# Another fixed order and other PSUM banks for the same 3284 tasks of a threshold-attention and mixer kernel

## The chip, the cores and the metric

The kernel runs on one core of one Trainium2 chip. The metric is the device time of one execution in microseconds, the median over runs; lower is better. Engines are named as in the profile: PE (matrix products; PEld its weight loads), DVE (vector), ACT (scalar), POOL (GpSimd), SP (sync, which here only issues DMAs).

## The reference

Attention over 8 batches, 8 heads, 576 rows, 64 columns, with a threshold in place of a plain softmax, and then a mixer with a low-rank part over the rows and two dense layers over 512 channels:

```python
scores = scale * np.matmul(q, k.transpose(0, 1, 3, 2))
thresh = np.max(scores, axis=-1, keepdims=True) - tau
scores = np.where(scores >= thresh, scores, -1000000000.0)
scores = scores - np.max(scores, axis=-1, keepdims=True)
attn = np.exp(scores)
attn = attn / (np.sum(attn, axis=-1, keepdims=True) + 1e-09)
x = np.matmul(attn, v)          # then heads side by side: (8, 576, 512)
...
xt = x.transpose(0, 2, 1)
h = xt @ U @ V                  # U: 576 x 32, V: 32 x 576
u = x + h.transpose(0, 2, 1)
out = u + np.maximum(u @ w_ch1, 0.0) @ w_ch2    # 512 -> 2048 -> 512
```

Inputs and output are fp32.

## The kernel before

**Pairs and steps.** Two heads of one batch are a pair; there are 32 pairs, numbered 0 to 31, four to a batch. The 576 rows of a head are four tiles of 128 and one of 64; the fifth tiles of two neighbouring pairs go together, so that two pairs have nine score steps. A score step writes two tiles of 128x576 scores (one for each head, j) into PSUM. Pairs 0 and 1, and the first step of every later two pairs, have single steps; else two steps are issued as one double step (`score_tasks`, L620).

**What one step goes through.** PE multiplies queries and keys in fp32 (L637); DVE scales a tile into SBUF and takes its minimum, since the sign is turned ("weighing", L666); ACT makes the threshold (L682) and the exponential (L689); DVE keeps what passes the threshold and sums it ("selection", L696). The weights are bf16; they are transposed by a DMA on SP's queue (L720) or, for some early tiles, by PE and an eviction on ACT (L727, L737), after POOL has copied their last 64 columns (L714). PE multiplies them with the values, which are split into a high and a low bf16 part (L796, L800, L804); DVE, ACT and POOL divide by the sums (L827, L851 to L862).

**Before a pair's first step** its queries and keys are loaded in eight parts (L506: five or four groups of 64 rows x 64 columns for 64 partitions, 80 or 64 KB), transposed by PE in fp32 (L568, L581) and copied to SBUF by ACT (L574, L587). Pairs 0 to 2 load mostly on SP's queue, later ones on POOL's. Values are loaded on SP's queue (L530).

**After a pair** come the low-rank products (L875, L890), the sum u on DVE (L897) and its transposition (L912 on PE for pairs 0 to 7, later by DMA). When the four pairs of a batch are done its mixer may start: 16 up-projections of four products (L994), with a relu on ACT (L984), and 16 down-projections of four (L1027), an addition on DVE (L1039) and the stores (L1050 to L1056). Odd batches carry the fifth tiles of two batches besides (L1010).

**What sets the order.** The work is cut into 3284 tasks, each with an engine, what it needs and a function that issues its instructions. They are numbered as they are made. `Order.run` (L352) goes through a table of numbers, `ORDER` (L130), and issues each task in that order; each engine so gets its own queue in the table's order, and semaphores hold an instruction until what it needs is there. A negative number issues an idle product of zeros into a bank (`fill`, L468): -3 into bank 2, -6 into bank 5.

```python
for n in ORDER:
    if n < 0:
        self.filler(-1 - n)
        continue
    t = self.tasks[n]
```

**Banks.** PSUM has eight banks. Banks 0 to 2 are the tile `trio0`, 3 to 5 `trio1`, 6 and 7 tiles of their own. A single score step takes banks 0, 1, 3 and 4, a double one 0 to 5. Every other task of PE that writes PSUM takes the one bank that the table `BANK` (L299) gives it. `BankOrder` (L10) makes the waits by banks: an access waits for the last access to the same bank from another engine.

Of the kernel before, what the change touches and what calls it, by code (L numbers as in the profile page):

```python
# [112 lines left out]
class Task:  # L113
# [17 lines left out]
    24, 22, 21, 26, 20, 23, 19, 25, 29, 42, 43, 28, 46, 27, -3, -3, -3, -3, -3, -3, -3, -3, -3, -3, -3, -3, -3, -3, 30, 39, 34, 31, 32,  # L131
    40, 35, 33, 45, -3, -3, 59, 41, 204, 60, 48, 61, 63, 205, -3, -3, -3, -3, -3, -3, 69, 62, 36, 47, 64, 65, 44, 37,
    70, 38, 203, 71, 73, 201, 1, 66, -3, -3, -3, -3, -3, -3, 82, 72, 199, 77, 3, 74, 202, 67, 52, 83, 200, 54, 50, 68,
    84, 86, 0, 78, -3, 95, 85, 90, 198, 87, 53, 208, 224, 51, 96, 55, 79, 88, 97, -3, -3, -3, 80, 75, 221, 76, 91,
    108, 98, 99, 2, 81, 49, 211, 109, 103, 89, 110, 104, -3, -3, -3, -3, 119, 111, 207, 219, 112, 220, 100, 114, 209,
    225, 120, 101, 121, 92, 102, 123, 222, 115, -6, -6, -6, -6, -6, 129, 125, 223, 113, 122, 218, 93, 130, 213, 118,
    94, 435, 131, 214, 212, 116, 439, 126, 117, 142, 132, 56, 434, 124, 137, 169, 57, 206, 143, 133, 58, 144, 146,
    168, 4, -6, 155, 210, 227, 138, 150, 127, 170, 229, 145, 433, 128, 156, 231, 105, 157, 437, 106, 232, 228, 438,
    151, 107, 238, 158, 226, 134, 163, 233, 230, 239, 456, 234, 159, -6, 171, 240, 135, 457, 136, 147, 241, 455, 173,
    164, 242, 459, 248, 160, 215, 458, 244, 165, 172, 139, 152, 174, 148, 250, 175, 436, 149, 140, 166, 249, 216, 161,  # L140
    217, 262, 251, 162, 256, 261, 167, 454, 245, 440, 273, 141, 432, 243, 252, 263, 257, 268, 246, 274, 264, 452, 247,
    275, -8, -8, 153, 258, 453, 176, 184, 253, 177, 442, 281, 183, 254, 154, 5, 286, 255, 277, 6, -4, 188, 185, 265,
    276, 259, 186, 260, 287, 266, 267, 189, 445, 282, 296, 446, 269, 283, 187, 291, 278, 288, 235, 447, 297, 284, 279,
    280, 289, 292, 236, 443, 285, 298, 441, 622, 190, 290, 619, 448, 302, 178, 306, 295, 345, 625, 444, 307, 293, 300,
    237, 294, 191, 344, 179, 192, 318, 308, 299, 626, 313, 346, 460, 301, 7, 180, 462, 319, 620, 309, 465, 270, 320,
    322, 624, 271, 303, 463, 466, 623, 181, 272, 310, 304, 321, 347, 464, 331, 311, 305, 182, 314, 326, 349, 348, 334,
    467, 315, 312, 193, 350, 316, 323, 351, 332, 317, 324, 461, -4, -4, 352, 642, 194, 353, 325, 640, 354, 327, 195,
    472, 646, 333, 355, 339, 8, 196, 335, 356, 468, 473, 197, -6, 357, 336, 328, 337, 621, 474, 364, 338, 9, 340, 476,
    482, 643, 475, 359, 358, 639, 477, 449, 341, 483, 478, 342, 450, 365, 329, 343, 484, 360, 330, 495, 485, 362, 486,
    496, 11, 498, 479, 645, 507, 497, 10, 487, 469, 480, 502, 363, 488, 361, 451, 508, 366, 634, 632, 509, 644, 511,  # L150
    627, 520, 367, 633, 629, 630, 368, 521, 635, 481, 631, 374, 886, 369, 499, 490, 530, 883, 370, 489, 523, 641, 491,
    371, 500, 532, 628, 515, 492, 372, 882, 501, 503, 493, 373, 470, 510, 376, 531, 494, 504, 525, 512, 13, 386, 377,
    887, 516, 378, 533, 534, 513, 541, 881, 514, 380, 387, 540, 12, 522, 379, 382, 375, 536, 524, 505, 383, 384, 535,
    506, 552, 381, 526, 543, 537, 527, 385, 553, 547, 471, 528, 650, 554, 542, 556, 388, 538, 565, 888, 539, 651, 390,
    560, 566, 517, 15, 394, 548, 885, 391, 529, 389, 544, 518, 555, 659, 572, 561, 545, 395, 396, 549, 568, 546, 661,
    16, 884, 660, 392, 397, 647, 557, 519, 550, 649, 669, 567, 393, 569, 551, 573, 570, 665, 670, 663, 562, 571, 578,
    558, 574, 671, 673, 398, 682, 677, 648, 683, 559, 579, 652, 672, 399, 654, 580, 402, 905, 678, 655, 662, 653, 563,
    14, 664, 575, 403, 400, 904, 564, 666, 901, 576, 694, 577, 902, 685, 674, 908, 401, 689, 695, 581, 892, 667, 684,
    696, 903, 896, 894, 893, 707, 582, 895, 1052, 708, 698, 675, 586, 679, 690, 668, 583, 599, 587, 897, 584, 636,
    691, 686, 585, 717, 676, 600, 697, 588, 710, 601, 589, 598, 709, 18, 699, 712, 17, 718, 590, 603, 700, 637, 701,  # L160
    719, 702, 638, 680, 727, 406, 604, 681, 602, 605, 890, 607, 728, 407, 606, 404, 608, 656, 687, 609, 906, 688, 713,
    692, 729, 591, 405, 1054, 765, 711, 592, 693, 907, 703, 734, 593, 610, 739, 594, 766, 714, 611, 657, 767, 715,
    704, 658, 595, 740, 723, 612, 716, 1048, 912, 752, 613, 720, 911, 596, 1055, 705, 735, 597, 408, 706, 741, 409,
    721, 724, 913, 614, 722, 410, 730, 615, 747, 725, 411, 736, 726, 731, 743, 914, 753, 616, 769, 732, 910, 742, 412,
    754, 915, 617, 891, 744, 773, 618, 733, 737, 770, 748, 745, 921, 774, 759, 764, 749, 889, 775, 755, 771, 794, 776,
    923, 746, 738, 772, 750, 414, 922, 1053, 751, 413, 756, 1049, 916, 917, 931, 795, 925, 760, 757, 927, 796, 1072,
    785, 758, 924, 932, 768, 786, 933, 761, 777, 909, 1050, 926, 415, 935, 1051, 942, 762, 1071, 787, 416, 934, 763,
    941, 1069, 778, 788, 1074, 417, 928, 779, 898, 1068, 780, 936, 946, 950, 929, 418, 944, 797, 930, 789, 781, 937,
    899, 951, 782, 900, 419, 790, 952, 960, 1061, 791, 1059, 954, 792, 783, 938, 793, 1063, 1062, 420, 943, 961, 918,
    421, 939, 947, 953, 1070, 940, 784, 422, 1064, 1277, 945, 1060, 956, 1274, 955, 1058, 970, 798, 1273, 957, 919,  # L170
    962, 963, 972, 1279, 965, 799, 971, 423, 948, 1278, 800, 949, 981, 974, 801, 1280, 426, 802, 973, 1275, 976, 424,
    806, 427, 958, 803, 1276, 959, 807, 1009, 975, 808, 977, 804, 428, 805, 966, 978, 429, 980, 985, 1075, 979, 809,
    1010, 1073, 811, 430, 982, 810, 1011, 431, 986, 989, 812, 964, 1056, 983, 967, 990, 920, 968, 813, 991, 993, 1013,
    999, 992, 814, 1057, 1000, 995, 425, 843, 994, 1004, 1079, 984, 1014, 969, 1081, 844, 1015, 1088, 1082, 987, 1008,
    988, 1080, 996, 1016, 1002, 815, 1089, 1001, 1077, 1012, 817, 1090, 816, 997, 1092, 1005, 998, 1017, 1091, 819,
    1003, 818, 1018, 1094, 1083, 1019, 1098, 1093, 1293, 1084, 820, 1028, 1020, 1095, 1297, 1021, 1006, 1100, 1065,
    1296, 821, 1007, 1099, 1294, 1037, 822, 1109, 1066, 1029, 1038, 1299, 1104, 1039, 1108, 1096, 1022, 1030, 1097,
    823, 1101, 1031, 1023, 1102, 1105, 1032, 1024, 1111, 1117, 1076, 1025, 824, 1295, 1078, 1103, 1113, 1067, 1118,
    1110, 1288, 1284, 1119, 1289, 1121, 1106, 1286, 1283, 1127, 845, 1285, 1107, 1446, 1128, 1120, 1287, 1033, 1447,
    1122, 1123, 1298, 1282, 1112, 1137, 1034, 1300, 1281, 846, 1114, 1441, 1130, 1035, 1040, 1085, 1138, 1440, 827,  # L180
    1132, 1139, 1086, 1141, 1442, 825, 1124, 828, 1115, 847, 1147, 1140, 1036, 1129, 1116, 826, 1148, 1125, 829, 1041,
    1133, 1126, 1143, 1156, 1131, 830, 1149, 1142, 1134, 848, 1152, 1157, 1087, 1135, 1304, 1150, 1158, 831, 1305,
    1443, 1166, 835, 1301, 1444, 1144, 1042, 1167, 1176, 1145, 1043, 836, 1146, 1151, 832, 1308, 1313, 1309, 1153,
    1159, 1162, 1154, 1177, 1306, 1315, 1160, 1155, 833, 1467, 1314, 1307, 1180, 1460, 834, 1163, 1136, 1169, 1445,
    1178, 1044, 1161, 1464, 1323, 1181, 1026, 1463, 1045, 1319, 1027, 1175, 1466, 1317, 1182, 1164, 1324, 1184, 1171,
    1179, 1165, 1204, 1325, 1183, 1168, 837, 1461, 1205, 1170, 1185, 839, 1186, 1327, 1206, 1187, 1333, 1462, 841,
    840, 1334, 838, 849, 1172, 1316, 842, 1320, 1173, 1342, 850, 1326, 1195, 1329, 1174, 1318, 1290, 1328, 1321, 1188,
# [975 lines left out]
```

## Time and profile before

| | |
|---|---|
| runs | 590.59, 591.26, 592.37 us; median 591.26 |
| the profiled execution's own time | 590.78 us |
| its span in the profile | 589.0 us |
| PE busy | 568.7 us, 97% |
| DVE busy | 509.9 us, 87% |
| ACT busy | 460.2 us, 78% |
| POOL busy | 331.7 us, 56% |
| chain of work that ended last | PE 56% of the span, DVE 2%, issue 1% |
| granted clock of PE in the 40 slices | 9 tenths or more in each |

The busy time of an engine counts its instructions and not its queue's. The ends of PE's products are modelled, so neighbouring ones overlap by some 0.17 us and an idle time of PE is shown too short. The waits are put down to what came last. Lines such as L637 are those of the kernel before; in the changed kernel the table is one line longer, so that L637 there is L638.

### The profile page before, as it was taken

The numbers are of one execution on the slowest core, as the hardware profiler recorded it, in microseconds if no ns is written. First come the engines' busy times: TensorE is split into PE (matmuls) and PEld (weight loads), VectorE is DVE, ScalarE is ACT, GpSimd is POOL, SyncE is SP. The second block draws the span as 40 slices with busy tenths as digits, with TensorE's granted clock in tenths as the row PEclk, the third lists the DMA queues.
The fourth block names the chain that finished last, engine by engine and source line by source line (L and its number), as shares of the span: only waits on it lengthen the run. The fifth ranks groups of instructions, "written<-read, shape, count | busy, mean of one in ns | idle before, by whom it ended". The sixth has DMA issues, their size and how long they took to land.

```text
span 589.0 us, 16929 instructions
## 1 busy us (share of the span) xinstructions
PE 568.7 (97%) x6142; PEld 345.8 (59%) x6214; DVE 509.9 (87%) x1400; ACT 460.2 (78%) x959; POOL 331.7 (56%) x580
## 2 busy tenths in 40 slices
PE   9898899999999999999999999999999999999996
PEld 3456655765666665555566665655665746556553
DVE  4999999999999999999998999999899799953101
ACT  4688999998899977998788987799877896774430
POOL 3887775968576748764666765566645551341000
PEclk9999999999999999999999999999999999999999
DMA  5999999969999999998989989999898798672303
GB/s 134 170 166 182 179 133 175 188 113 176 193 155 186 147 173 203 165 175 166 159 166 173 188 147 198 162 188 186 142 175 165 122 167 168 134 117 46 72 1 90
DMA packets 226996, 90.49 MB, mean 154 GB/s; under 512 B 205408, under 2 KB 217520, under 8 KB 226912
## 3 DMA queue, kind: packets, MB, share of 16 engines
q1 hardware_dynamic: 212544, 67.48, 70.5%
q0 software_dynamic: 13408, 21.58, 19.8%
q8 instruction: 49, 0.80, 0.6%
q10 hardware_dynamic: 960, 0.34, 0.2%
q14 instruction: 35, 0.29, 0.2%
HBM read 37.90 MB, written 9.44 MB: 80 GB/s over the span
## 4 chain that ended last, share of the span: by engine, by line
PE 56%; DVE 2%; issue 1%; ACT 0%
PE trio L637 13%; PE bank L1027 12%; PE trio L994 6%; PE bank L994 6%; PE trio L1027 4%; PE bank L800 4%; PE trio L800 3%; PE bank L1010 1%; PE bank L568 1%; PE trio L568 1%; DVE s_sb L666 1%; PE bank L875 1%; DVE w_ring L696 1%; PE bank L796 0%; PE trio L1010 0%
## 5 line engine op out<-in xcount | busy, mean ns | idle before, releaser
L689 ACT ACTIVATE e_sb<-s_sb,m 128x576 bf16<-128x576 f32 x288 | 217.5, 774 | 37.2 <-DVE s_sb L666 18.0
L696 DVE SCALAR_TENSOR_TENSOR w_ring<-s_sb,thr,e_sb 128x576 bf16<-128x576 f32 x288 | 229.7, 823 | 5.5 <-issue 1.5
L666 DVE TENSOR_SCALAR_CACHE_REDUCE s_sb<-trio 128x576 f32<-128x576 f32 x288 | 205.3, 749 | 9.3 <-PE trio L637 8.5
L637 PE MATMUL trio<-qkT 64*64 64x288 f32 (+2 forms) x2304 | 161.8, 410 | 2.1 <-DVE s_sb L666 1.6
L714 POOL COPY w_ring<-w_ring 128x128 bf16<-128x128 bf16 (+1 forms) x168 | 65.0, 395 | 115.3 <-DVE w_ring L696 71.7
L637 PEld LDWEIGHTS trio<-qkT 64*64 64x64 f32 x2304 | 81.4, 133 | 52.9 <-DVE s_sb L666 6.4
L1027 PE MATMUL bank<-W2b,R 128*128 128x512 bf16 x402 | 101.6, 380 | 1.9 <-issue 0.6
L506 POOL DMA_DIRECT2D qkraw<-in_k_dram x117 | 76.6, 656 | 25.9 <-PE trio L568 12.0
L1027 PEld LDWEIGHTS <-R 128*128 128x128 bf16 x576 | 53.1, 98 | 60.8 <-issue 9.1
L506 POOL DMA_DIRECT2D qkraw<-in_q_dram x117 | 76.4, 655 | 12.0 <-PE bank L581 3.0
L994 PEld LDWEIGHTS <-W1b 128*128 128x128 bf16 x512 | 46.7, 98 | 55.9 <-issue 10.9
L862 POOL TENSOR_TENSOR x<-x,rec 128x256 f32<-128x256 f32 (+1 forms) x84 | 52.7, 631 | 33.0 <-DVE x L855 21.8
L984 ACT ACTIVATE R<-bank 128x512 bf16<-128x512 f32 x80 | 47.2, 594 | 29.6 <-PE bank L994 16.4
L994 PE MATMUL bank<-uT,W1b 128*128 128x512 bf16 x244 | 66.6, 380 | 1.8 <-DVE x L855 0.2
L603 POOL TENSOR_TENSOR vh<-vraw_ring,vh 64x128 bf16<-64x128 f32 x64 | 53.5, 835 | 19.1 <-ACT vh L596 9.5
L800 PEld LDWEIGHTS <-wT_ring 128*128 128x128 bf16 x896 | 55.5, 98 | 9.9 <-issue 3.6
L994 PE MATMUL trio<-uT,W1b 128*128 128x512 bf16 x231 | 57.6, 379 | 0.4
L984 ACT ACTIVATE R<-trio 128x512 bf16<-128x512 f32 x64 | 37.5, 597 | 8.4 <-PE trio L994 8.0
L682 ACT ACTIVATE thr<-m,tau_t 128x2 f32<-128x2 f32 x144 | 41.5, 293 | 2.3 <-DVE s_sb L666 1.9
L1039 DVE TENSOR_TENSOR o<-bank,x 128x512 f32<-128x512 f32 x27 | 18.5, 686 | 27.5 <-PE bank L1027 27.2
L800 PE MATMUL bank<-vh,wT_ring 128*128 128x128 bf16 x496 | 35.6, 220 | 0.1
L1027 PE MATMUL trio<-W2b,R 128*128 128x512 bf16 x140 | 33.5, 379 | 0.3
(105 smaller groups left out, 719.6 us busy)
## 6 DMA issues: line engine op xcount, KB each, us to landing
out_dram<-o SPq DMA_DIRECT2D x71, 128.0 KB, 2.9
vraw_ring<-in_v_dram SPq DMA_DIRECT2D x32, 160.0 KB, 4.0
qkraw<-in_k_dram POOLq DMA_DIRECT2D x59, 80.0 KB, 4.2
qkraw<-in_q_dram POOLq DMA_DIRECT2D x58, 80.0 KB, 4.5
vraw_ring<-in_v_dram SPq DMA_DIRECT2D x32, 128.0 KB, 4.1
qkraw<-in_q_dram POOLq DMA_DIRECT2D x59, 64.0 KB, 4.2
qkraw<-in_k_dram POOLq DMA_DIRECT2D x58, 64.0 KB, 4.3
W1b<-in_moe_w_ch_dram POOLq DMA_DIRECT2D x8, 256.0 KB, 5.5
```

Of the source, the lines that this page charges most:

```text
L506: queue.dma_start(pr.qkraw[part, to, j, :], src[:, j, of, :])
L603: nc.gpsimd.tensor_tensor(out=pr.vh[part, tiles_, :, h, :], in0=raw[part, tiles_], in1=pr.vh[part, tiles_, :, 0, :], op=ALU.subtract)
L637: mm = nc.tensor.matmul(cols[part, lo:hi], a.tT[hs, 0, rows], a.tT[hs, 1, lo:hi], start=True, stop=True)
L666: nc.vector.tensor_scalar(out=s_sb, in0=score_cols(slot, x), scalar1=-scale, scalar2=None, op0=ALU.mult, op1=ALU.min, accum_out=m[:, x:x + 1])
L689: nc.scalar.activation(out=e_sb, in_=s_sb, func=ACT.Exp, bias=m[:, x:x + 1], scale=-1.0)
L696: nc.vector.scalar_tensor_tensor(out=w_sb[:, 0:S], in0=s_sb, scalar=thr_[:, x:x + 1], in1=e_sb, op0=ALU.is_le, op1=ALU.mult, accum_out=pr. ...
L714: nc.gpsimd.tensor_copy(out=w_sb[:, xs, S:640], in_=w_sb[:, xs, 512:S])
L800: nc.tensor.matmul(av[:, 2 * a + j, :], w, pr.vh[:, kt, j, :, :], start=kt == 0, stop=False)
L862: nc.gpsimd.tensor_tensor(out=x, in0=x, in1=over_sum(part), op=ALU.mult)
L984: nc.scalar.activation(out=R2[:, fts, lo:hi], in_=bank[t.got[0]].rearrange("p (f c) -> p f c", c=hi - lo), func=ACT.Relu)
L994: nc.tensor.matmul(bank[t.got[0]], W1b[:, dt, ft * P:(ft + 1) * P], bt.uT[:, dt, :], start=(dt == 0), stop=(dt == 3))
L1027: nc.tensor.matmul(ch, R2[:, ft, lo:lo + P], W2b[:, ft, :], start=(ft == 0), stop=(ft == 15))
```

## The change

The two tables are replaced. `ORDER` holds the same 3284 tasks, each of them moved by 13 places on average and by up to 289; 45 idle products instead of 49, 11 of them ahead of the first transposition instead of 14. `BANK` gives another bank to 277 of the 481 tasks that have one. All else is the same line for line: the tasks, what each needs, tiles, buffers, DMAs.

```diff
 ORDER = (
-    24, 22, 21, 26, 20, 23, 19, 25, 29, 42, 43, 28, 46, 27, -3, -3, -3, -3, -3, -3, -3, -3, -3, -3, -3, -3, -3, -3, 30, 39, 34, 31, 32,
...
+    25, 22, 21, 26, 19, 23, 20, 24, 46, 44, 29, 28, 40, -3, -3, -3, -3, -3, -3, -3, -3, -3, -3, -3, 30, 27, 32, 31, 34, 39,
...
 BANK = {n: b for b, tasks in {
     0: (
...
-        2449, 2496, 2514, 2635, 2665, 2817, 2819, 2825, 2837, 2849, 2857, 2906, 3190, 3224, 3228,),
...
+        2402, 2408, 2415, 2417, 2433, 2437, 2665, 2685, 2778, 2825, 3003, 3057, 3183, 3198, 3203, 3224, 3232, 3234,),
```

What it moves is read from the engines' queues. The names: `trio_159` and `trio_160` are trio0 and trio1, `bank_161` and `bank_162` banks 6 and 7; `qkraw_103` holds the raw queries and keys of even pairs, `qkraw_104` of odd ones; `qkT_105` and `qkT_106` the transposed ones; `w_ring` the weights; `R_163` the relu's output.

PE's queue between the first and the second score step of pair 1, before:

```order
L637 MATMUL trio_160<-qkT_106 64x288 x2
L568 MATMUL trio_159<-ident,qkraw_103 128x128 x4
L469 LDWEIGHTS zeros
L469 MATMUL trio_160<-zeros 128x512
...
L637 MATMUL trio_159<-qkT_106 64x288 x2
```

and now:

```order
L638 MATMUL trio_160<-qkT_106 64x288 x2
L569 MATMUL bank_161<-ident,qkraw_103 128x128 x4
L470 LDWEIGHTS zeros
L470 MATMUL trio_159<-zeros 128x512
L728 LDWEIGHTS w_ring_82
L728 MATMUL bank_162<-identb,w_ring_82 128x128
...
L638 MATMUL trio_159<-qkT_106 64x288 x2
```

Before, the pair of idle rows stands five times; now once, and the weight transposition's pair of rows five times. The query transpositions of pair 2 (the x4 row) stay; the key ones, which stood ahead of the first score step, are now behind the third.

SP's queue where the last query loads of pair 2 stand, before:

```order
L506 DMA qkraw_103<-in_k_dram 64x5x64
L506 DMA qkraw_103<-in_q_dram 64x4x64 x2
L506 DMA qkraw_103<-in_k_dram 64x4x64
L506 DMA qkraw_103<-in_q_dram 64x5x64
L720 DMA_TRANSPOSE wT_ring_84<-w_ring_80 128x10x128
L506 DMA qkraw_103<-in_q_dram 64x5x64
L530 DMA vraw_ring_88<-in_v_dram 64x2x64
```

and now:

```order
L507 DMA qkraw_103<-in_k_dram 64x5x64
L721 DMA_TRANSPOSE wT_ring_84<-w_ring_81 128x5x128
L507 DMA qkraw_103<-in_q_dram 64x5x64
L507 DMA qkraw_103<-in_q_dram 64x4x64
L721 DMA_TRANSPOSE wT_ring_84<-w_ring_80 128x10x128
L507 DMA qkraw_103<-in_k_dram 64x4x64
L531 DMA vraw_ring_88<-in_v_dram 64x2x320
L507 DMA qkraw_103<-in_k_dram 64x4x64
```

The last query load, 24th DMA of the queue, stood behind the ten-block transposition; now the last query load is the 23rd, behind a five-block one, and two key loads stand behind the ten-block one.

PE's queue at the end of pair 7's scores and, further on, before the second score step of pair 8, before:

```order
L875 MATMUL bank_162<-xb_ring_99,Ub 128x128
L568 MATMUL bank_161<-ident,qkraw_104 128x128 x4
L912 LDWEIGHTS ub_151
L912 MATMUL trio_159<-identb,ub_151 128x128
...
L727 MATMUL bank_162<-identb,w_ring_82 128x128
...
L1027 MATMUL bank_161<-W2b,R_163 128x512
L581 MATMUL trio_160<-ident,qkraw_104 128x128
L637 MATMUL trio_159<-qkT_105 64x288 x2
```

and now:

```order
L876 MATMUL bank_162<-xb_ring_99,Ub 128x128
L569 MATMUL bank_161<-ident,qkraw_104 128x128 x4
L1028 LDWEIGHTS R_163
L1028 MATMUL trio_159<-W2b,R_163 128x512
...
L728 MATMUL bank_161<-identb,w_ring_82 128x128
...
L582 MATMUL trio_159<-ident,qkraw_104 128x128
L801 LDWEIGHTS wT_86
L801 MATMUL bank_162<-vh_108,wT_86 128x128
...
L638 MATMUL trio_159<-qkT_105 64x288 x2
```

The weight transposition (L727) used the bank of the low-rank product (L875) shortly before; now it uses the bank of the fp32 transpositions, with twelve products of 512 columns (L1028) between. The transposition L581 stood right ahead of the double step; now ten small products stand between.

## Rows read from the trace of the kernel before

**Rows 1.** Busy time by stage; columns: stretch, its length, each engine's busy time, clock.

```profile
9.00:83.00 74.00, 64.92 (x962) 41.21 (x955) 71.64 (x201) 62.13 (x124) 57.32 (x105) 1.00 1.12 168
83.00:140.00 57.00, 55.96 (x642) 35.23 (x648) 55.92 (x156) 54.73 (x115) 42.00 (x77) 1.00 1.05 160
140.00:500.00 360.00, 356.35 (x3892) 220.30 (x3946) 345.05 (x951) 299.67 (x636) 216.66 (x371) 1.00 0.99 169
```

**Rows 2.** Timeline of PE, 78 to 84 us: start, duration, instruction, idle before.

```profile
83.07 1.02 PE L994 MATMUL bank<-uT,W1b 128*128 128x512 bf16 x3 [0.18 <-ACT uT L928]
```

**Rows 3.** Waits of DVE, 0 to 84 us: total, times, longest.

```profile
DVE s_sb L666 <- PE trio L637: 7.0, 2, 6.3
DVE x L827 <- PE bank L796: 0.4, 1, 0.4
```

**Rows 4.** Waits of PE, 140 to 589 us.

```profile
PE bank L1027 <- issue: 0.6, 4, 0.2
```

**Rows 5.** Timeline of PE at the opening.

```profile
0.99 4.85 PE L469 MATMUL trio<-zeros 128*128 128x512 bf16 x11 [0.99 <-DVE tau_t L397]
...
0.99 5.50 PE L469 MATMUL trio<-zeros 128*128 128x512 bf16 x14 [0.99 <-DVE tau_t L397]
...
6.33 0.61 PE L568 MATMUL trio<-ident,qkraw 128*128 128x128 f32 x4
```

**Rows 6.** DMA issues at 2.4 us: size, time to landing.

```profile
qkraw<-in_q_dram SPq DMA_DIRECT2D x1, 80.0 KB, 3.7
```

**Rows 7.** Timeline of PE, 15 to 48 us.

```profile
24.25 0.63 PE L568 MATMUL trio<-ident,qkraw 128*128 128x128 f32 x4 [0.78 <-issue]
...
24.71 1.24 PE L469 MATMUL trio<-zeros 128*128 128x512 bf16 x5
...
25.88 1.20 PE L637 MATMUL trio<-qkT 64*64 64x288 f32 x16
...
37.93 2.17 PE L637 MATMUL trio<-qkT 64*64 64x288 f32 x32
```

**Rows 8.** Timeline of DVE, 15 to 48 us.

```profile
23.28 0.07 DVE L696 DVE_READ_ACCUMULATOR w_ring<-s_sb,thr,e_sb 128x1 f32 x1
...
23.50 0.76 DVE L666 TENSOR_SCALAR_CACHE_REDUCE s_sb<-trio 128x576 f32<-128x576 f32 x1
...
27.12 0.76 DVE L666 TENSOR_SCALAR_CACHE_REDUCE s_sb<-trio 128x576 f32<-128x576 f32 x1 [0.69 <-PE trio L637]
...
39.72 0.74 DVE L666 TENSOR_SCALAR_CACHE_REDUCE s_sb<-trio 128x576 f32<-128x576 f32 x1
```

**Rows 9.** Timeline of SP's queue, 14 to 28 us.

```profile
16.55 2.30 SPq L720 DMA_TRANSPOSE wT_ring<-w_ring  x1
...
18.89 0.93 SPq L506 DMA_DIRECT2D qkraw<-in_q_dram  x1
...
20.63 1.23 SPq L720 DMA_TRANSPOSE wT_ring<-w_ring  x1
```

**Rows 10.** DMA issues at 18.9 us.

```profile
qkraw<-in_q_dram SPq DMA_DIRECT2D x1, 80.0 KB, 5.3
```

**Rows 11.** Timeline of PE, 119 to 137 us.

```profile
120.59 0.39 PE L912 MATMUL trio<-identb,ub 128*128 128x128 bf16 x4
...
121.28 0.44 PE L727 MATMUL bank<-identb,w_ring 128*128 128x128 bf16 x5 [0.30 <-ACT tt L881]
...
130.57 0.27 PE L581 MATMUL trio<-ident,qkraw 128*128 128x128 f32 x1
...
131.03 2.17 PE L637 MATMUL trio<-qkT 64*64 64x288 f32 x32 [0.19 <-DVE s_sb L666]
...
135.30 1.03 PE L1027 MATMUL bank<-W2b,R 128*128 128x512 bf16 x4
...
136.44 0.45 PE L875 MATMUL trio<-xb_ring,Ub 128*128 128x128 bf16 x5
```

**Rows 12.** Busy time by stage, the first idle products; last columns: clock, DMA share, GB/s.

```profile
0.90:5.60 4.70, 4.61 (x11) 1.66 (x12) 2.17 (x12) 1.49 (x2) 1.75 (x4) 1.00 0.59 140
```

385 rows, old and new, of tables (BANK, ORDER) are left out of this document.

## The prediction

> **What bounds the kernel now.** I read the busy time by stage first [rows 1]. From 9 to 83 us DVE is busy 71.64 of 74 us and PE 64.92; from 140 to 500 us PE is busy 356.35 of 360. So there are two stages. Up to 83.07 us, where the first up-projection of the mixer stands [rows 2], PE has only attention to work on and goes at DVE's pace; from there it has a store of mixer products and is the bound to the end. The tables of waits then say what is lost in each. DVE waits 7.0 us for scores in the first 84 us, of which 6.3 are the opening, so 0.7 later, and 0.4 us once for a product [rows 3]. After 140 us PE's longest entry is 0.6 us in four waits [rows 4].
>
> This bounds what any order of the same tasks can give. All products, evictions and loads stay. PE idles much before 83 us, but it gets work there only as fast as DVE makes selections; taking PE's waits away gives nothing unless DVE moves up. What is to be had is DVE's 74 − 71.64 = 2.4 us up to 83, PE's 57 − 55.96 = 1.0 us up to 140 [rows 1], the 0.6 us after that and a few tenths in the opening: some 4 us, 0.7% of the time.
>
> **The opening: 11 idle products, and other first loads.** Eleven idle products take 4.85 us and all fourteen 5.50 us from 0.99 us; the first transposition starts at 6.33 [rows 5]. Three products less free PE by 0.65 us. But that transposition also needs the last query load of pair 0, issued at about 2.4 us and 3.7 us under way [rows 6]: 6.1 us. With the same load at most 0.2 us is free. The change puts the 64 KB part last instead of the 80 KB part, which can land earlier: the upper bound is 0.6 us. Against it, two 80 KB loads of pair 1 follow at once where a 32 KB one stood; as lower bound I allow 0.2 us the other way. I take 0.1, since the load and not PE is last. In all the program has 45 idle products and not 49; the others stand before the first up-projection in PE's spare time, so they cost and give nothing while DVE is the pace there; if it were not, four at 0.21 us, 0.8 us.
>
> **The late query load of pair 2.** This is the one large loss of DVE's stage. After the first score step of pair 1 PE stands at the query transpositions of pair 2 until 24.25 us, 0.78 us idle for nothing that the profile names; behind them come five idle products from 24.71, and only then, at 25.88, the next score step [rows 7]. DVE idles 0.69 us until 27.12 for that step, and 0.15 us (23.28 + 0.07 to 23.50) for the one before [rows 8]. The cause is on SP's queue: the load was issued at 18.89, behind a DMA transposition of ten blocks that held SP 2.30 us from 16.55 [rows 9], and took 5.3 us [rows 10]: 24.2 us.
>
> Three things move here. The last query load stands one place earlier on SP, behind a transposition of five blocks and not of ten (1.23 us in place of 2.30 [rows 9]), so I put its issue 1.1 + 0.4 us earlier, near 17.4, and its landing, again 5.3 us later, near 22.7. The key transpositions of pair 2, which stood ahead of the first score step of pair 1, now stand behind the third. And of five idle products between the query transpositions and the second score step one is left, with the five small products of a weight transposition. The first step then starts when DVE releases it, before 22.0, and ends (1.20 us) near 23.2; 0.5 us of transpositions, 0.2 and 0.3 us later PE is at the second step, at 24.2. DVE needs two weighings of at most 0.76 us from 23.3 to release its banks, so PE is no longer last, and the 0.69 + 0.15 = 0.84 us go. Bounds: nothing, if the load is as late as before; 1.2 with the 0.4 us for a product [rows 3]. I take 0.84, as the issue moves by more than PE's 0.78 us of waiting. What is late next there is DVE itself. This moves up the first up-projection and all that PE does after.
>
> **Waits of PE from 83 to 140 us.** Three have one pattern: a product writes a bank that ACT or DVE still reads. At 121.28 a weight transposition waits for the copy of a low-rank product of the same bank, with 0.7 us of PE work between; at 131.03 a double score step stands right behind a transposition into one of its own banks; at 136.44 a low-rank product uses a bank of the score steps [rows 11]. The ends there are modelled, so I count from start to start, a product of 512 columns at 0.21 us (five take 1.24, four 1.03 [rows 7, 11]), a small one at 0.06 (0.45 less 0.39), a transposition of fp32 at 0.11: 0.45, 0.35 and 0.3 us, 1.1 in all; the idle listed is 0.5. In the change twelve products of 0.21 us stand ahead of that weight transposition, ten small ones between that transposition and the double step, and the low-rank product has another bank. All three should go. A new order has waits of its own: between 0.1 us (57 us of the stretch after, 0.6 us in 449) and 1.1. I take 0.4, nearer to the long quiet stretch. Net 0.7; bounds 1.0 and 0.
>
> **After 140 us** the same is allowed for the new order, 0.6 us [rows 4], so the difference is nothing, with 0.6 us either way. The end is the same in both: the last products, a sum, two stores.
>
> **The sum.** 0.1 + 0.84 + 0.7 = 1.64 us off the profiled execution's own 590.78 us: 589.14. The median of the runs is 591.26, 0.48 above it; carried over, 589.6 us, 0.28% less than the median. A measurement of this kernel can tell about 0.3% (1.8 us) from no change, so this is no change, by a hair.
>
> **Row and rule on the clock.** The first eleven idle products take 0.44 us each and the three behind them 0.22 (5.50 less 4.85, over three) [rows 5]: TensorE's lower level, 1.2 GHz, and then 2.4. The granted clock of those first 4.7 us is listed as 1.00 all the same [rows 12], so the pitch is the better witness here. PE had worked on nothing but these products when the level rose. The eleven that stay are the slow ones, at the same moments, so I take the rise for unchanged: no term in the sum. The Trainium skill, page "TensorE: Matmul & The Clock Gate", section on the HAM clock gate, has it that the number of slow products at the start differs between runs of one kernel (6, 11 or 14 seen). By that rule some runs would miss the three products that go; one trace can't show it.
>
> **The rivals.**
> - *The late load only moves* (same, 590.4). PE stands at pair 2's queries again, or at its keys, whose last two loads now stand behind the ten-block transposition. For it: such a load took 5.3 us where the opening's took 3.7 [rows 6, 10]. Against: the keys have two score steps more time. It costs the 0.84: 589.6 + 0.84.
> - *Most small waits go* (faster, 588.0). If the new order is quiet everywhere, 0.2 + 1.2 + 1.0 and the 0.6 us of the rest go, 3.0 us, and with the opening's upper bound 3.4: 591.26 − 3.0 to 3.4, about 588.0. Against: DVE is busy 55.92 of 57 us from 83 to 140 [rows 1], so it would soon stop PE.
> - *Score steps come too late for DVE* (slower, 593.3). Four double steps of the change before 83 us have only some 1.4 us of DVE work (two selections) between the weighing that frees their last bank, or the one before it, and the weighing that reads them; 2.1 us and more stood there. If a double step (2.17 us [rows 7]) could only start after it, DVE would idle 0.7 us at each, 2.8 in all: 591.26 + 2.8 less the 0.1 and 0.7 of the other parts. It decides from the point where a step waits for its last bank before its first product. Against: a weighing starts at 39.72, 1.8 us into the step from 37.93 and before its end [rows 7, 8], so steps and weighings overlap by parts.
> - *The clock rises later* (same, 592.0). Nine transpositions (0.11 us each) and the first step (1.20) at half speed add some 2.2 us ahead of DVE's first weighing; with the load's gain still there, 589.6 + 2.2 = 591.8, and a few tenths of idle products more. No row speaks for it.
>
> **How the numbers follow.** The forecast 0.50, the load that only moves 0.20, most waits gone 0.20, late steps 0.08, the clock 0.02. Of the forecast's half two fifths lie under the bound of 589.5, as it stands so near: faster 0.20 + 0.20 = 0.40; within 0.3%: 0.30 + 0.20 + 0.02 = 0.52; slower 0.08. The range goes from 587.7, 0.3 below the rival of few waits, to 591.8, which is the moved load with 1.1 us of new waits and 0.3 of scatter; outside lie the late steps, the clock and a tenth more.
>
> **What would show it.** In the changed kernel's trace: the first transposition near 6.2 us; the second score step of pair 1 near 25 us and no idle DVE behind it; the first up-projection near 82.1 us instead of 83.07; listed waits of PE from 84 to 140 us under 0.5 us; after 140 us as few as now. A first up-projection at 83 or later would say that the load or the score steps took the gain; one at 82.1 with the end unmoved, that new waits of PE gave it back.

## The result and the profile after

The changed kernel took 600.47 us (median of six executions, 593.72 to 602.86), the kernel before on the same chip 591.69 (590.59 to 594.03): a ratio of 1.0124, interval 1.0094 to 1.0154. It is slower by 1.2%, where no change was forecast, and its executions lie over 9 us where those of before, here, lie over 3.4. The ratios, here and below, leave out executions more than 1.5% above the shortest of the same kernel; medians and spreads keep them, and the profiled executions of e8 and e10 are of that kind.

The execution that was profiled is the shortest of the six: 593.72 us, span 591.9, against 590.78 and 589.0 before. So its trace holds some 3 us of the loss and not the rest. Its busy time by stage, to set against [rows 1]:

```profile
9.00:83.00 74.00, 66.80 (x960) 42.88 (x952) 72.23 (x201) 61.69 (x123) 54.61 (x104) 1.00 1.08 164
83.00:140.00 57.00, 55.76 (x638) 35.23 (x642) 54.91 (x154) 54.20 (x114) 43.99 (x77) 1.00 1.00 162
140.00:500.00 360.00, 358.52 (x3934) 219.48 (x3927) 347.26 (x950) 300.18 (x634) 222.24 (x369) 1.00 0.98 169
```

DVE is busier up to 83 us (72.23 for 71.64), as was wanted, and less busy from 83 to 140 (54.91 for 55.92), where PE was to gain: 55.76 for 55.96. PE's timeline at the three places that were forecast ([rows 5, 7, 2]):

```profile
1.00 3.88 PE L470 MATMUL trio<-zeros 128*128 128x512 bf16 x11 [1.00 <-DVE tau_t L398]
6.66 0.63 PE L569 MATMUL trio<-ident,qkraw 128*128 128x128 f32 x4 [1.78 <-DMA qkraw<-in_q_dram]
...
25.06 1.20 PE L638 MATMUL trio<-qkT 64*64 64x288 f32 x16 [0.47 <-DVE s_sb L667]
...
83.66 1.02 PE L995 MATMUL bank<-uT,W1b 128*128 128x512 bf16 x4 [0.19 <-ACT uT L929]
```

The first transposition waits for a query load and is 0.33 us later. The second score step of pair 1 comes at 25.06, as forecast, for 25.88. Yet the first up-projection is at 83.66 and not 82.1; before it was 83.07. What PE waits for from 84 to 141 us is now:

```profile
PE trio L728 <- POOL w_ring L715: 0.8, 1, 0.8
PE trio L801 <- DVE s_sb L667: 0.2, 1, 0.2
PE bank L995 <- ACT uT L929: 0.2, 1, 0.2
```

That is 1.2 us, for under 0.5 expected. One thing the prediction never looked at stands in the table of instructions of the tile W2b, the mixer's second weights, eight loads of 256 KB on POOL's queue (count, duration in ns, first and last start). Before:

```profile
L1090 POOL DMA_DIRECT2D W2b<-in_moe_w_ch_dram x8: 716/744/768, 72.5 to 112.3; - x8
```

and after:

```profile
L1091 POOL DMA_DIRECT2D W2b<-in_moe_w_ch_dram x8: 716/723/777, 90.8 to 113.4; - x8
```

The first of them starts 18 us later, the last 1 us later. The table of DMA issues from 90 to 102 us (count, size, median us to landing) shows the crowd. Before:

```profile
W2b<-in_moe_w_ch_dram POOLq DMA_DIRECT2D x2, 256.0 KB, 7.2
...
wT_ring<-w_ring SPq DMA_TRANSPOSE x4, 7.9
```

after:

```profile
W2b<-in_moe_w_ch_dram POOLq DMA_DIRECT2D x5, 256.0 KB, 6.5
...
wT_ring<-w_ring SPq DMA_TRANSPOSE x4, 9.4
```

Five loads in place of two, and the transpositions of the selections, which SP issues, land after 9.4 us and not 7.9. That the place of these loads makes the loss became the theory that the experiments settled, but only after two others.

### The profile page after: what moved, and what is told of

Read it like the earlier page. It is cut to its first block, busy times and chain, and to the rows that moved or that the text cites. A ratio compares the mean times of both kernels' runs of the same rounds, so it can differ in the third digit from the quotient of the medians.

```text
span 591.9 us, 17011 instructions
## 1 busy us (share of the span) xinstructions
PE 574.1 (97%) x6210; PEld 347.2 (59%) x6210; DVE 512.4 (87%) x1400; ACT 461.3 (78%) x959; POOL 335.7 (57%) x580
## 5 line engine op out<-in xcount | busy, mean ns | idle before, releaser
L667 DVE TENSOR_SCALAR_CACHE_REDUCE s_sb<-trio 128x576 f32<-128x576 f32 x288 | 206.0, 750 | 12.8 <-PE trio L638 10.9
L715 POOL COPY w_ring<-w_ring 128x128 bf16<-128x128 bf16 (+1 forms) x168 | 67.2, 407 | 97.7 <-DVE w_ring L697 78.6
L638 PEld LDWEIGHTS trio<-qkT 64*64 64x64 f32 x2304 | 83.7, 132 | 53.1 <-issue 8.0
L1028 PE MATMUL bank<-W2b,R 128*128 128x512 bf16 x400 | 96.4, 379 | 0.0
L1028 PEld LDWEIGHTS <-R 128*128 128x128 bf16 x576 | 53.0, 98 | 63.2 <-issue 11.1
L995 PEld LDWEIGHTS <-W1b 128*128 128x128 bf16 x512 | 45.9, 98 | 57.2 <-issue 12.1
L604 POOL TENSOR_TENSOR vh<-vraw_ring,vh 64x128 bf16<-64x128 f32 (+1 forms) x64 | 53.8, 841 | 32.6 <-ACT vh L597 13.2
L995 PE MATMUL bank<-uT,W1b 128*128 128x512 bf16 x272 | 68.4, 380 | 0.2 <-ACT uT L929 0.2
L995 PE MATMUL trio<-uT,W1b 128*128 128x512 bf16 x240 | 59.7, 379 | 0.4 <-DVE s_sb L667 0.4
L985 ACT ACTIVATE R<-trio 128x512 bf16<-128x512 f32 x65 | 38.3, 597 | 12.1 <-PE trio L995 10.9
L1028 PE MATMUL trio<-W2b,R 128*128 128x512 bf16 x176 | 41.7, 379 | 0.3 <-ACT R L985 0.3
L801 PE MATMUL bank<-vh,wT_ring 128*128 128x128 bf16 x544 | 39.0, 219 | 0.0
L797 PE MATMUL bank<-vh,wT_ring 128*128 128x64 bf16 x164 | 31.6, 193 | 0.0
```

Of the source, the lines that this page charges most:

```text
L604: nc.gpsimd.tensor_tensor(out=pr.vh[part, tiles_, :, h, :], in0=raw[part, tiles_], in1=pr.vh[part, tiles_, :, 0, :], op=ALU.subtract)
L638: mm = nc.tensor.matmul(cols[part, lo:hi], a.tT[hs, 0, rows], a.tT[hs, 1, lo:hi], start=True, stop=True)
L667: nc.vector.tensor_scalar(out=s_sb, in0=score_cols(slot, x), scalar1=-scale, scalar2=None, op0=ALU.mult, op1=ALU.min, accum_out=m[:, x:x + 1])
L715: nc.gpsimd.tensor_copy(out=w_sb[:, xs, S:640], in_=w_sb[:, xs, 512:S])
L801: nc.tensor.matmul(av[:, 2 * a + j, :], w, pr.vh[:, kt, j, :, :], start=kt == 0, stop=False)
L985: nc.scalar.activation(out=R2[:, fts, lo:hi], in_=bank[t.got[0]].rearrange("p (f c) -> p f c", c=hi - lo), func=ACT.Relu)
```

## The experiments

All ratios are to the kernel before, run beside them. Where a kernel is put together from two orders, the place at which one goes over into the other is called a joint.

**First four: opening or order.** The changed kernel again; with 14 opening idle products; the kernel before with 11; and before's order up to the first score step of pair 2 with the change behind it.

```diff
 # e2, to the changed kernel (e3 is the mirror)
-    28, 40, -3, -3, -3, -3, -3, -3, -3, -3, -3, -3, -3, 30,
+    28, 40, -3, -3, -3, -3, -3, -3, -3, -3, -3, -3, -3, -3, -3, -3, 30,
 # e4, at the joint: before, then the change
-    226, 436, 134, 238, 163, 438, 151, 158,
+    438, 151, 107, 238, 432, 171, 139, 226,
```

> The changed kernel as it is, for the spread of its executions and the granted clock of each. Theory 1 (opening): PE is idle 1.8 us between the 11 idle products and the first transposition, and how long TensorE then stays at its lower level differs from execution to execution; the times spread over 593 to 603 us and the slower ones have a mean granted clock of 0.993 to 0.997. Theory 2 (order): new waits on loads and banks cost the time; the times spread, but the clock does not go with them.

> The changed kernel with 14 opening idle products again, nothing else. Theory 1: every execution at a mean clock of 0.999 or more, 592 to 594 us, so 7 us of the loss go and 1 to 3 us stay with the order. Theory 2: as the changed kernel, about 600 us.

> The kernel before with 11 opening idle products, nothing else. Theory 1: executions with a clock under 0.998, some of them 4 to 9 us over 591.7, median 596 to 600 us. Theory 2: 591 to 592 us as before.

> Order and banks of the kernel before up to the first score step of pair 2 (14 idle products among them, about 34 us), the changed order and banks after it. Theory 1: 590 to 593 us with a clock of 0.999 or more. Theory 2 with the cost spread over the program: 598 us or more; with the cost in the first 34 us: 591 to 592 us.

| | median, spread (us) | ratio, interval |
|---|---|---|
| e1, the change again | 597.34, 593.91 to 601.46 | 1.0107, 1.0065 to 1.0149 |
| e2, change with 14 idle | 597.31, 593.75 to 611.28 | 1.0088, 1.0055 to 1.0121 |
| e3, before with 11 idle | 592.48, 590.84 to 598.84 | 1.0031, 1.0005 to 1.0058 |
| e4, before up to 34 us | 599.37, 594.48 to 602.13 | 1.0124, 1.0083 to 1.0166 |

The loss repeats. Fourteen idle products do not give it back; eleven cost the kernel before some 0.3%, at the edge of what can be told. The opening and the first 34 us are not it. In e1 the mean granted clock does fall with the time, from 0.999 at 593.91 us to 0.994 at 600.84, as theory 1 would have it; but so it does in e2, with fourteen idle products (0.989 at 611.28 us), so the opening is not what lowers it. e1's trace, of an execution of 595.82 us, lost more than the first one at two places, near 98 and near 435 us; for the first, its table of DVE's waits from 84 to 141 us has

```profile
DVE w_ring L697 <- DMA wT_ring<-w_ring: 1.6, 1, 1.6
```

A selection may only write its buffer once the transposition that read it has landed. Before, this wait was 0.5 us in two. Landings from 90 to 102 us were later than the 9.4 of the first trace, too: 10.9 us in the median in e1 and e2, 9.6 in e4.

**Where along the program.** Before's order and banks up to a score step, the change's behind it; and the mirror. Each keeps its banks, but for transpositions that would clash at the joint.

```diff
 # e5, first step of pair 5 (83 us)
-    502, 521, 881, 530, 523, 370, 883, 491,
+    369, 499, 490, 530, 470, 641, 881, 523,
 # e6, first step of pair 10 (163 us)
-    984, 1014, 1001, 1088, 425, 1004, 994, 987,
+    1081, 844, 1015, 1088, 1076, 1008, 1012, 1082,
 # e7, first step of pair 20 (320 us)
-    2104, 1625, 2248, 2114, 1954, 1613, 2246, 1970,
+    2244, 1954, 1970, 2114, 1260, 2083, 1833, 1937,
 # e8: the change up to pair 10, then before (shown to before)
-    1081, 844, 1015, 1088, 1082, 987, 1008, 988,
+    984, 1014, 1001, 1088, 419, 1275, 425, 994,
```

> The order and banks of before up to the first score step of pair 5 (some 83 us), those of the change behind it. Theory A (the time is lost up to 163 us: by waits of the new order while DVE sets the pace or just after): the part lost up to 83 us goes, the rest stays, 594 to 596 us. Theory B (it is lost behind 163 us, in the long stretch in which PE is the bound, and in most executions more than in the profiled ones): 597 to 600 us, as the changed kernel.

> The order and banks of before up to the first score step of pair 10 (some 163 us), those of the change behind it. Theory A: about 592 us (591.3 of before and up to 1 us of single waits). Theory B: 597 to 600 us.

> The order and banks of before up to the first score step of pair 20 (some 320 us), those of the change behind it. Theory A: 591 to 592 us. Theory B: 594 to 597 us if the loss is spread over the stretch; 597 to 600 if it all lies behind 320 us; 591 to 592 if it all lies from 163 to 320 us.

> The mirror of e6: the order and banks of the change up to the first score step of pair 10, those of before behind it. Theory A: 597 to 600 us, as the changed kernel. Theory B: 591.5 to 593 us.

| | median, spread (us) | ratio, interval |
|---|---|---|
| e5, before up to 83 us | 594.91, 593.47 to 596.64 | 1.0065, 1.0047 to 1.0083 |
| e6, before up to 163 us | 593.20, 591.70 to 597.35 | 1.0034, 1.0017 to 1.0050 |
| e7, before up to 320 us | 595.17, 593.54 to 597.26 | 1.0067, 1.0049 to 1.0085 |
| e8, the change up to 163 us | 601.44, 593.79 to 604.12 | 1.0102, 1.0066 to 1.0138 |

e8 carries the whole loss, e6 little of it: theory A holds in the main, most of the loss arises up to 163 us. From e4 to e5, which differ by the order from 34 to 83 us, 3.5 us go by the ratios. e5 has in its part of before the first load of W2b, so that one fewer stands in the crowd, and its transpositions from 90 to 102 us land after 5.9 us; what it still loses is not theirs. e6, which keeps before's order and loads up to 163 us, still loses 2.0 us by its ratio, so theory A is not the whole: some of the loss, or the joint's cost, lies behind 163 us. e7 lies in the range that theory B gave for a loss spread over the stretch, and against A. But it has less of the change than e6 and loses more, and its trace waits 1.7 us around its own joint (four entries of PE from 318 to 345 us), so it is no witness for the stretch behind it.

e8's profiled execution took 603.33 us, one of its longest, and its trace shows the loss at its largest: PE starts its first up-projection at 83.77, as the others, and DVE is 11 us behind at 136. Its DMA issues from 90 to 102 us:

```profile
W2b<-in_moe_w_ch_dram POOLq DMA_DIRECT2D x5, 256.0 KB, 11.0
...
wT_ring<-w_ring SPq DMA_TRANSPOSE x4, 12.5
```

DVE's longest waits from 84 to 141 us:

```profile
DVE w_ring L696 <- DMA wT_ring<-w_ring: 4.5, 3, 2.7
DVE w_ring L696 <- ACT wT_ring L737: 2.9, 1, 2.9
DVE w_ring L696 <- POOL w_ring L714: 1.8, 1, 1.8
```

and PE's:

```profile
PE bank L800 <- DMA wT_ring<-w_ring: 3.1, 1, 3.1
PE bank L727 <- DVE x L855: 2.8, 2, 1.5
```

The largest of each hang directly on transpositions of w_ring that land late, DVE for its buffer and PE for its operand. One more cost follows from PE's idleness; by stage (the clock is the third number from the end):

```profile
118.00:122.00 4.00, 2.96 (x40) 2.33 (x41) 3.29 (x10) 3.16 (x7) 2.32 (x4) 1.00 1.31 121
122.00:126.00 4.00, 1.47 (x16) 0.84 (x12) 1.85 (x6) 3.02 (x8) 3.58 (x7) 1.00 1.56 110
126.00:130.00 4.00, 3.46 (x34) 2.80 (x37) 3.15 (x6) 1.34 (x3) 2.51 (x6) 0.58 1.32 176
```

After a stretch with 1.47 us of work in four the granted clock is 0.58 over the next four: the lower of its two levels (1.2 and 2.4 GHz) for some 3.4 of them, the higher for the rest, while PE has work for 3.46.

**The crossed pair: loads alone.** Six numbers of the table moved in the change, eight in before; nothing else.

```diff
 # e9, to the changed kernel: six loads of W2b (11 to 16)
-    527, 381, 13, 552, 537,
-    390, 566, 11, 389, 648, 15, 556, 544,
-    660, 549, 14, 572, 661,
-    550, 570, 12, 578, 551,
-    600, 712, 16, 601, 710,
+    496, 480, 11, 507, 485,
+    504, 500, 12, 525, 885,
+    378, 517, 13, 514, 387,
+    565, 545, 14, 518, 555,
+    573, 558, 15, 393, 569,
+    671, 574, 16, 673, 571,
 # e10, to the kernel before: the same loads where the change has them
+    537, 527, 13, 385, 553,
+    388, 538, 11, 15, 565,
+    396, 549, 14, 568, 546,
+    558, 574, 12, 671, 673,
+    586, 679, 18, 16, 690,
+    636, 691, 17, 686, 585,
```

> The changed kernel with the first six loads of the second mixer weights (256 KB each, line L1091) put at places of POOL's queue near those of before (some 76, 84, 89, 95, 99 and 102 us), where the change has five of them from 90.8 to 100.6 us; nothing else is moved. Theory A1 (these loads crowd the transfers of 90 to 130 us, and the DMA transpositions of the selections land late): 593 to 595 us, the spread of the runs under 5 us, landings of the transpositions issued from 90 to 110 us under 9 us. Theory A2 (it is the order and the banks of PE's work in that stretch): 597 to 600 us as before the edit, spread 7 us or more.

> The mirror: the kernel before with the eight loads of the second mixer weights behind the same twin copies of POOL as in the change (five from some 91 to 101 us, three at some 110 us), nothing else moved. Theory A1: 595 to 599 us with a spread of 5 us and more. Theory A2: 591.5 to 592.5 us.

e9: 592.71 us, 591.92 to 595.39, ratio 1.0022 (1.0006 to 1.0038). e10: 600.05 us, 594.66 to 605.50, ratio 1.0100 (1.0059 to 1.0141). So the places of the loads make the loss in either order, and spreading them takes most of it away in the change; A2 falls. Both times lie outside A1's ranges, on the side that makes the loads more important. The tables of DMA issues from 90 to 102 us, e9:

```profile
W2b<-in_moe_w_ch_dram POOLq DMA_DIRECT2D x3, 256.0 KB, 6.0
...
wT_ring<-w_ring SPq DMA_TRANSPOSE x5, 6.4
```

e10 (its execution took 604.95 us, one of its longest; the median of the loads is as in e9, but the one issued at 98.72 took 11.4 us and the next, at 103.15, 12.6):

```profile
W2b<-in_moe_w_ch_dram POOLq DMA_DIRECT2D x4, 256.0 KB, 6.2
...
wT_ring<-w_ring SPq DMA_TRANSPOSE x2, 12.1
```

and, from 84 to 141 us, e10's longest waits of DVE for transpositions and of PE for POOL:

```profile
DVE w_ring L696 <- DMA wT_ring<-w_ring: 6.8, 3, 4.5
PE trio L727 <- POOL w_ring L714: 2.7, 1, 2.7
```

**What the pair does not part.** A load takes two things: its transfer, and some 0.72 us of POOL's own queue, in which the copies stand that PE's weight transpositions need. Both ways show. PE's wait of 0.8 us in the first trace of the change, at 127.11 us, is for such a copy, and there POOL works without a listed gap from 111 to 130 us. In e9 one load fewer stands just ahead, the copy is done some 2 us earlier, and the wait is gone:

```profile
126.03 1.02 POOL L715 COPY w_ring<-w_ring 128x128 bf16<-128x128 bf16 x2
...
124.56 0.48 POOL L714 COPY w_ring<-w_ring 128x128 bf16<-128x128 bf16 x2
```

e10's 2.7 us, at 97.25, come behind three loads. The waits for transpositions themselves are 1.6 us in e1, and 4.5 and 6.8 in the long executions of e8 and e10. That the places of the loads are the cause is shown; how much of it goes by late transfers and how much by POOL's queue is read from these traces and was not tried apart.

With the crowd gone, e9's row of 83 to 140 us shows what the order itself does there:

```profile
83.00:140.00 57.00, 56.41 (x651) 35.76 (x657) 55.82 (x157) 55.32 (x115) 42.01 (x80) 1.00 1.08 169
```

PE is busy 56.41 us for 55.96 before, and its listed waits are two of 0.2 us. e9 is 0.86 us late at the first up-projection (83.93 for 83.07) and only 0.14 us late at the first weighing of pair 10. So 0.45 us by the one measure and 0.7 by the other came, of 0.7 forecast for this stretch.

**Where the 0.84 us of the late load went.** DVE's weighings do move up: with the opening 0.36 us late in e9, the last one of the second score step of pair 1 is 0.44 early, a gain of 0.80. A few weighings on, at 33.80, e9 is 1.02 late. In the changed kernel's timeline of DVE:

```profile
27.08 0.75 DVE L667 TENSOR_SCALAR_CACHE_REDUCE s_sb<-trio 128x576 f32<-128x576 f32 x1
...
30.93 2.33 DVE L697 SCALAR_TENSOR_TENSOR w_ring<-s_sb,thr,e_sb 128x576 bf16<-128x576 f32 x1
```

The same selection before:

```profile
31.75 0.77 DVE L696 SCALAR_TENSOR_TENSOR w_ring<-s_sb,thr,e_sb 128x576 bf16<-128x576 f32 x1
```

It takes 1.5 us more, though its exponential was done at 29.08 and its threshold at 29.26. POOL at that time, in the changed kernel:

```profile
30.78 0.67 POOL L507 DMA_DIRECT2D qkraw<-in_q_dram  x1
31.46 1.17 POOL L604 TENSOR_TENSOR vh<-vraw_ring,vh 128x512 bf16<-128x512 f32 x1
```

e11 takes the change only up to 30 us (with 14 idle products); e12 moves that subtraction in e9.

```diff
 # e11, joint at the third step of pair 1 (shown to before)
-    439, 126, 117, 142, 132, 56, 434, 124,
+    4, 133, 124, 142, 208, 211, 213, 94,
 # e12, to e9
-    208, 150, 58, 170, 231,
+    143, 127, 58, 128, 212,
```

> The order and banks of the change up to the third score step of pair 1 (some 30 us: with it the late query load of pair 2 and what was moved around it), with 14 opening idle products; those of before behind it. By the forecast's term for the late load all behind it moves up 0.8 us: 590.3 to 590.8 us, first up-projection near 82.3 us. By the rival that the gain is lost at the next wait for a selection (1.3 us at 33 us in the changed kernel's trace): 591.3 to 592.5 us, first up-projection at 83 us or later.

> e9 with one more edit: POOL's subtraction of 512 columns for the values of pair 1 (line L603, 1.17 us, some 31.7 us) moved up behind the twin copy that stands before it, ahead of two loads. Theory P (the late load's 0.8 us was gained and then lost because a selection of DVE stands still, 2.33 us in place of 0.81, while POOL works there): that selection takes 0.8 to 0.9 us, the first up-projection comes near 82.4 to 82.7 us (83.93 in e9), 591.2 to 591.7 us. Theory Q (the selection is long for another reason, such as the banks or the loads around it): it stays at 2.3 us, 592.7 us.

e11: 592.15 us, 591.22 to 594.43, ratio 1.0005 (0.9988 to 1.0022), first up-projection at 83.61: on the side of the rival, that the gain is lost at the next selection. That selection starts at 31.81 beside the same subtraction and takes 1.71 us. e12's timeline, DVE and POOL:

```profile
31.41 0.76 DVE L696 SCALAR_TENSOR_TENSOR w_ring<-s_sb,thr,e_sb 128x576 bf16<-128x576 f32 x1
```

```profile
30.06 1.15 POOL L603 TENSOR_TENSOR vh<-vraw_ring,vh 128x512 bf16<-128x512 f32 x1
```

With the subtraction out of its way the selection takes 0.76 us, and the weighings behind it, up to 42 us, are 0.34 us or more earlier than before where e9's were up to 1.03 later. Theory P holds for the cause. Its time does not come: 591.93 us, ratio 1.0026 (0.9992 to 1.0059), with executions from 590.44 to 602.50, five of the twelve over 594 us. (The kernel before, run beside it 29 times, spread nearly as far, from 589.84 to 598.75, but with only four over 594.) e12's shortest is 0.6 us above the shortest of before beside it, e9's 1.5: a difference of the size of the gain, no more than a hint. The profiled execution took 597.27, with the first up-projection at 88.79. Its row for 30 to 50 us, and e9's:

```profile
30.00:50.00 20.00, 16.75 (x219) 10.76 (x219) 17.21 (x52) 13.97 (x28) 15.91 (x28) 0.83 1.19 171
```

```profile
30.00:50.00 20.00, 16.26 (x274) 10.87 (x273) 19.97 (x56) 16.07 (x32) 15.67 (x30) 1.00 1.24 171
```

DVE, busy 19.97 of 20 us in e9, idles 2.8 here, all of it for one score step. That step, here and in e9:

```profile
43.32 4.12 PE L637 MATMUL trio<-qkT 64*64 64x288 f32 x32 [1.48 <-ACT wT_ring L737]
```

```profile
43.02 2.24 PE L637 MATMUL trio<-qkT 64*64 64x288 f32 x32 [0.55 <-ACT wT_ring L737]
```

PE has waited 1.3 us for a copy of POOL and 1.5 for an eviction of ACT, and starts only 0.3 us later than in e9; then the step takes 1.9 us more, as the granted clock of these 20 us is 0.83, so that some 7 of them were at the lower level. POOL's copies come behind a wait of 1.45 us that is put down to a key load. The transpositions issued from 28 to 48 us land after 8.3 us in the median, 6.4 in e9 and 5.6 in the changed kernel's trace; but 7.3 before, which lost nothing by it. So a late load stands ahead of the loss as far as the trace tells, and the clock makes most of it. Over e12's executions, too, the five over 594 us have mean clocks of 0.991 to 0.996, the seven others 0.998 or more.

**Keeping what gains.** e13 puts the change from 83 to 163 us, with e9's loads, into the kernel before; e14 adds e12's start up to 40 us and 14 idle products; e15 is e12 with three loads of the first weights (W1b) moved up.

```diff
 # e13, joints at pairs 5 and 10 (e14: also at 248, the double step of pair 2)
+    369, 499, 490, 530, 470, 641, 881, 523,
...
+    984, 1014, 1001, 1088, 419, 1275, 425, 994,
 # e15, to e12
-    357, 338, 7, 340, 482, 476, 8, 475, 359,
-    355, 328, 9, 339, 335,
+    299, 293, 7, 284, 300,
+    272, 304, 8, 623, 305,
+    332, 315, 9, 192, 311,
```

> The kernel before up to the first score step of pair 5 (some 83 us), the change with the spread loads of e9 up to that of pair 10 (some 163 us), the kernel before behind it. If the change's gain of 0.7 us in PE's waits from 84 to 141 us, seen in e9, holds by itself: 590.5 to 591.0 us. If the two joints cost as much as it gives: 591.3 to 592.5 us.

> All that seems to gain, with 14 opening idle products: the change with e12's edits up to the double score step of pair 2 (some 40 us), the kernel before up to pair 5, the change with spread loads up to pair 10, the kernel before behind it. If the 0.7 us of the late load and the 0.7 us of 84 to 141 us add: 589.6 to 590.5 us, faster than both kernels. If the joints take it: 591 to 592.5 us.

> e12 with three loads of the first mixer weights (256 KB each, line L1087) moved up too, from 70 to 73 us to some 56, 60 and 65 us. If the loads that crowd at 70 to 78 us are what makes most of e12's executions longer than its best (590.4 us): median 590.4 to 591.2 us and few runs over 593. If it is the stretch from 30 to 50 us, where its trace already lost 2.2 us on late transpositions: as e12, 591.5 to 592.5 us with runs up to 600 us.

e13: 592.56 us, ratio 1.0004 (0.9979 to 1.0029); e14: 591.26, ratio 1.0002 (0.9979 to 1.0025); both as before. In e13's trace a gain of some 0.8 us is there up to 141 us, but the first joint costs 1.7 us (PE's waits, 83 to 90 us), and behind the second PE waits another 1.1:

```profile
PE bank L727 <- POOL w_ring L714: 1.7, 1, 1.7
```

e15 is a miss: 594.98 us, ratio 1.0047 (1.0018 to 1.0076). With the loads at 58.5, 62.5 and 68.2 us it again loses 2.9 us from 36 to 49 us. The transpositions issued at 30.0 and 35.3 us took 10.6 and 8.6 us, POOL and PE wait as in e12, and the same score step takes 3.86 us, at a granted clock of 0.91 from 30 to 50 us. So the crowd at 70 us is not what spreads e12's executions; what makes the transfers of 30 to 50 us late in some of them stays open. No version beats the kernel before.

## Why the prediction was wrong

**What bounds the kernel** was right as far as it went: DVE up to 83 us [rows 1, 2, 3], PE behind it. It did not count the transfers as a third bound, though the DMA share was a column of its first rows: 1.12 and 1.05 [rows 1]. The share alone would not have told, though: e9, which loses little, has 1.13 and 1.08.

**The step that failed** is the term for the stretch from 83 to 140 us: "A new order has waits of its own: between 0.1 us … and 1.1. I take 0.4". It was bounded by PE's waits in the old order, so it could not hold a wait for a transfer, or for POOL's copies behind the loads, that the old order did not make late. The loads of the second mixer weights had moved by up to 18 us on POOL's queue, and the prediction followed only the query loads on SP's. Measured, the piece that the loads make is the difference of the changed kernel's ratio, 1.0107 to 1.0124, and e9's, 1.0022: 0.85 to 1.0%, some 5 to 6 us, where 0.4 was put down for all new waits. The Trainium skill, page "DMA: Bandwidth & Descriptors", section "Issuing engines are not separate DMA queues", says that transfers started by different engines run on the same 16 DMA engines and interleave. The runs agree: with POOL's loads close together SP's transpositions from 90 to 102 us landed after 9.4 us (the change) and 10.9 (e1), with the loads spread after 6.4 (e9).

**Opening, −0.1.** Nothing that can be told from scatter: PE was done with the idle products at 4.88 us and waited 1.78 for a query load [rows 5, 6], and DVE's first weighing came 0.07 to 0.36 us later than in the trace of before with the change's opening (after, e1, e8, e9), 0.04 to 0.55 later with before's own (e5, e6, e7, e10).

**The late load, −0.84** [rows 7 to 10]. The mechanism was right, and 0.80 us came, at the place named. The sentence "What is late next there is DVE itself" missed what came next on DVE: a selection slowed from 0.8 to 2.33 us by POOL. e12 shows the cause by taking it away; in its profiled execution, and it may be in the other long ones, the gain is then lost at the next place.

**PE's waits, −0.7 net** [rows 11, 4]. Right in itself, within what can be told: e9 gains 0.45 us of PE's busy time from 83 to 140 us, 0.7 us of lateness up to 163, once the loads stand apart.

**After 140 us, 0, with 0.6 us either way.** This term was too small as well. e9 shows some 1.2 us of loss there: 0.14 us late at pair 10, 1.4 at the end of its span. e6, the change from pair 10 on alone, loses 0.34%, 2.0 us, its joint included. PE's timeline has its gaps near 316, 340, 362 and 561 us, in every version with the change's late part.

**The clock** [rows 12]. The eleven idle products took 3.88 us and not 4.85, so the level rose among them, earlier than in the trace of before; no term needed it. Its role was elsewhere, behind long waits, as in e8 and e12.

**The rivals.** None was the one that came. "Score steps come too late" gave the nearest time, 593.3, which would have been luck, as its wait is not there: DVE waits for scores 6.9 us up to 84 us, of which 6.3 are the opening, as before [rows 3].

## What to carry to other kernels

When an order moves, follow every large transfer on every queue, not only those near the known waits, and ask what lands beside it: here eight loads that are needed only at 121 us set the time by when they were issued. A load moved is also a piece of the issuing engine's queue moved, and what stands behind it there waits. A trace of one short execution can understate what a kernel costs: the first one held 3 us of the 9. Look at the spread over executions beside it, and at that of the kernel before, which was 3.2 to 8.9 us in the rounds here. And a gain for the engine that sets the pace is only worth what the next thing beside it allows, here another engine's subtraction and then waits behind which the clock falls.

## What the runs showed of the hardware that was not expected

How late a transposition by DMA lands depends on the places of other loads: with the same order of everything else the median from 90 to 102 us went from 9.4 us (the change) and 10.9 (e1) to 6.4 (e9) by the places of six 256 KB loads on another queue, and from 7.9 (before) to 12.1 in the long execution of e10 by eight. It is not the count alone: in e5 four such loads start from 89.8 to 100.9 us, 3.4 us or more apart, and the median is 5.9; in the changed kernel three start within 3 us. In e8's long execution the loads of queries, keys and values issued from 90 to 130 us were late as well, 8.6 to 16.0 us (medians by size and tensor), 3.1 to 8.7 before. A late landing need not cost: e6 has 8.9 us in that stretch and loses nothing there.

A selection of DVE (two inputs in SBUF) that meets a subtraction of POOL (also from SBUF) can be slowed from 0.8 to 2.33 us and ends about 0.6 us after POOL does (33.26 for 32.63). Most such meetings cost the selection little: in the changed kernel 19 selections overlap a subtraction of this line and no other computing of POOL, 0.90 us on average, this one among them. At least once it is POOL that pays: at 331.75 a small subtraction that meets two selections, of 0.80 and 0.81 us, takes 1.56 us, where one of the same size at 114.22 took 0.42. The Trainium skill, page "SBUF — State Buffer", section "Who interferes with whom", has DVE instructions with two SBUF inputs contend with POOL's reads and says that whoever issues first keeps the port. The traces agree that one holds up the other; on the order they are divided. In e11 POOL was first, 31.76 for 31.81, and DVE waited; at 331.75 DVE was first, at 331.47, and POOL waited; both as the page has it. But at 30.93 in the changed kernel DVE was first by the recorded starts, POOL came at 31.46, and DVE was still the one that waited, which stays open. POOL's DMA issue ahead of the subtraction does not do it alone: in e12 the selection starts at 31.41 beside such an issue (31.16 to 31.86) and takes 0.76.
